# Moving the loads of a fused attention and FFN kernel behind the q transposes, and attention ahead of the FFN

## The chip, the cores and the metric

One core of one Trainium2 chip. The metric is the device time of one execution in microseconds, median of several runs; lower is better. Ratios below are computed as the mean time of one kernel's fast runs over that of the kernel before in the same rounds on the same chip, so they are not quite the ratio of the medians that are quoted beside them.

## The reference, cut to what matters

```python
# q, k, v: (8 batches, 8 heads, 576 tokens, 64); w_phi: (64, 128)
proj = x @ w_phi;  proj -= max(abs(proj), axis=-1)        # phi of q and of k
phi = concat([exp(proj), exp(-proj)])
kv = phi(k)^T v;  z = sum over tokens of phi(k)
x = (phi(q) kv) / (phi(q) z)                              # attention, 4608 tokens x 512
out = relu(x @ w_in)**2 @ w_out                           # FFN 512 -> 2048 -> 512
```

## The kernel before

The program has its own planner. It describes each piece of work as an operation with an engine, an estimated cost, a key (priority) and dependencies, runs a greedy list schedule over all engines once, and emits the instructions of each engine in the order found. On the chip every engine works through its own list in that fixed order; semaphores only guard data. **So a dependency that stands only in the plan (as on loads) changes an order, but the chip does not wait for it.**

```python
def load(key, kb, rows, fn, deps=(), bufs=()):            # HBM to SBUF, issued by GpSimd
    ...
    i = pl.op("pool", 780, key, fn, list(deps) + ..., bufs, lat=0)
    d = pl.op("dma", kb * 2.5, key, None, [i], bufs, lat=2600)

def xbar(key, kb, fn, deps=(), bufs=()):                  # DMA transpose, issued by SyncE
    i = pl.op("sp", 1300, key, fn, deps, bufs, lat=0)
    return pl.op("xb", kb * 6, key, None, [i], bufs, lat=2500)
```

For batches 2 to 7, k and q are loaded from the chip's memory (HBM) to the core's (SBUF) as they lie, and five DMA transposes each make kT and qT (for q from batch 1). The output x of attention is turned into xT, the FFN's input, by further DMA transposes, all from SyncE's one queue:

```python
nc.sync.dma_start_transpose(out=xt.t[:, u0 // 2 : (u0 + n) // 2, :], in_=...)   # kT, qT
nc.sync.dma_start_transpose(out=xT.t[:, tt], in_=xo.t)                         # xT
```

The K phase of a batch (phi of its k) costs VectorE, for each of two banks of PSUM, the memory that takes matmul results, in five groups, a reduce and a subtract (`mk`, `ksh`):

```python
def less(e, ...):
    amax(e)                                               # reduce: mk
    nc.vector.tensor_tensor(out=ksh..., in0=wv(e), in1=mk..., op=ALU.subtract)
```

FFN work is cut into 288 units (four 512-column matmuls each) whose keys are 0, 1, 2, ...; a batch of attention gets keys in a window of SPAN units that ends DUE units before the FFN needs it. NATT is how many of the 8 PSUM banks attention may hold; LEAD, a planner constant for pacing attention.

```python
NATT, LEAD, DUE, SPAN = 7, 3, 26, 36
def place(b):
    ...
    end = due[(NJ * b + NJ - 1) // 2 // 4] - DUE
    return lambda i: end - SPAN * (1 - i / 100)
...
attention(b, ... loads(b, last_x[b - 2][-2] if b > 3 else None), place(b))
```

Of the kernel before, what the change touches and what calls it, by code (L numbers as in the profile page):

```python
# [10 lines left out]
BF16 = mybir.dt.bfloat16  # L11
# [34 lines left out]
class Plan:  # L46
# [31 lines left out]
    def order(self):  # L78
        ready = {e: [] for e in sorted({o.eng for o in self.ops}, key=lambda e: (e != "x", e))}
        busy = {e: 0.0 for e in ready}  # L80
        rows = {e: None for e in ready}
        for o in self.ops:
            if o.n == 0:
                heapq.heappush(ready[o.eng], (o.key, o.seq, o))
        ev, now, done = [], 0.0, []

        def can(o):
            new = [x for x in o.bufs if x.slot is None]
            return all(x.can() and len(x.ring.free) >= sum(y.ring is x.ring for y in new)
                       for x in new)  # L90

        while True:
            for e, q in ready.items():
                if busy[e] > now:
                    continue
                skip = []
                while q:
                    it = heapq.heappop(q)
                    o = it[2]
                    if not can(o):  # L100
                        skip.append(it)
                        continue
                    for x in o.bufs:
                        if x.slot is None:
                            x.take()
                    o.start = now
                    end = now + o.cost
                    if o.rows is not None:
                        if rows[e] not in (None, o.rows):
                            end += self.SWITCH  # L110
                        rows[e] = o.rows
                    busy[e] = end
                    done.append(o)
                    same = [d for d in o.next if d.eng == e]
                    other = [d for d in o.next if d.eng != e]
                    for i, (t, what) in enumerate((
                            (end, ()), (end + 60, same), (end + o.lat, other),
                            (end + o.lat, None))):
                        heapq.heappush(ev, (t, 4 * o.seq + i, o, what))
                    break  # L120
                for it in skip:
                    heapq.heappush(q, it)
                if busy[e] <= now and e in self.idle and self.idle[e][2].start is None:
                    cost, fn, _ = self.idle[e]
                    o = Op()
                    o.eng, o.fn, o.start, o.cost, o.key = e, fn, now, cost(now), 1e9
                    busy[e] = now + o.cost
                    done.append(o)
                    heapq.heappush(ev, (busy[e], -len(done), o, ()))
            if not ev:  # L130
                break
            now = ev[0][0]
            while ev and ev[0][0] <= now:
                _, _, o, what = heapq.heappop(ev)
                if what is None:
                    for x in o.bufs:
                        x.left -= 1
                        if x.left == 0:
                            x.ring.free.append(x.slot)
                    continue  # L140
                for d in what:
                    d.n -= 1
                    if d.n == 0:
                        heapq.heappush(ready[d.eng], (d.key, d.seq, d))
        assert all(o.start is not None for o in self.ops)
        self.span = now
        return done
# [10 lines left out]
def kernel(  # L158
# [10 lines left out]
    nc = tc.nc  # L169
# [4 lines left out]
    P = 128  # L174
# [3 lines left out]
    M = U // 2  # L178
# [16 lines left out]
    wphi_f = sb.tile([P, Fd], F32, name="wphi_f")  # L195
    ones = sb.tile([P, Fd], BF16, name="ones")
    scrap = sb.tile([P, 8], F32, name="scrap")

    r_xk = ring("xk", 2, [P, U, D], BF16)
    r_xq = ring("xq", 2, [P, U, D], BF16)  # L200
# [16 lines left out]
    r_h2 = ring("h2", 30, [P, TCH], BF16)  # L217
    r_ot = ring("ot", 2, [P, DM], F32)

    NATT, LEAD, DUE, SPAN = 7, 3, 26, 36  # L220

    r_one = ring("one", 8, [P, 512], F32, ps)
    r_att = Ring(list(range(NATT)))
# [2 lines left out]
    pl = Plan()  # L226
# [15 lines left out]
    def pool(key, cost, fn, deps=(), bufs=()):  # L242
        return pl.op("pool", cost, key, fn, deps, bufs, lat=150 + MARGIN)

    queue, issues = [], []
# [8 lines left out]
    def load(key, kb, rows, fn, deps=(), bufs=()):  # L254



        n = (queue[-1][0] if queue else 0) + rows
        full = [d for m, d in queue if m >= n - 4096][:1]
        i = pl.op("pool", 780, key, fn, list(deps) + (full if n > 4096 else []), bufs, lat=0)  # L260
        issues.append(i)
        d = pl.op("dma", kb * 2.5, key, None, [i], bufs, lat=2600)
        queue.append((n, d))
        return d

# [75 lines left out]
    def attention(b, x, key):  # L341
# [4 lines left out]
        def transposes(xb, ld, xt, at):  # L346

            ops = []
            if b >= NPE or b and at:
                for u0, n in GRP:  # L350
                    def fn(u0=u0, n=n):
                        nc.sync.dma_start_transpose(
                            out=xt.t[:, u0 // 2 : (u0 + n) // 2, :],
                            in_=xb.t[:, u0 : u0 + n, :].rearrange("x u d -> x (u d)"),
                        )
                    ops.append(xbar(key(at), n * 16, fn, ld[0] + (x["v"][1][0] if b > 1 else []), [xb, xt]))
                return ops
            for u0, n in ((0, 16), (16, 16), (32, 4)) if b or at else GRP:
                w, = banks(1)

                def fn(u0=u0, n=n, w=w):
                    for i in range(n // 2):
                        nc.tensor.transpose(
                            out=tp(w)[:, i], in_=xb.t[:, u0 + 2 * i : u0 + 2 * i + 2, :]
                            .rearrange("x u d -> x (u d)"), identity=ident)
                kk = key(1 + u0 + 4 * at)
                p_ = pe(kk, 40 + n * 30, fn,
                        [o_id] + ld[0] + (ld[-1] if u0 + n > U // 2 else []), [w, xb, xt])
                ms = slice(u0 // 2, (u0 + n) // 2)
                if b or at:  # L370
                    o = dve(kk, n * 38, lambda w=w, n=n, ms=ms: nc.vector.tensor_copy(
                        out=xt.t[:, ms, :], in_=tp(w)[:, : n // 2]), [p_], [w, xt])
                else:
                    o = act(kk, n * 64, lambda w=w, n=n, ms=ms: nc.scalar.activation(
                        out=xt.t[:, ms, :], in_=tp(w)[:, : n // 2], func=ACT.Copy),
                        [p_], [w, xt])
                ops += [o] * (1 if not (b or at) else (n + 7) // 8)
            return ops

        tk = transposes(xk, lk, kT, 0)  # L380
        tq = transposes(xq, lq, qT, 1)


        va = [Buf(r_va), Buf(r_va)] if b == 0 else [Buf(r_va)] * 2
# [134 lines left out]
        for i, (g0, j0, nj) in enumerate(order_j):  # L519
# [117 lines left out]
            if hi_ == P and b == 0:  # L637
                w, = banks(1)

                def fn(w=w, xo=xo):  # L640
                    for kc in range(KC1):
                        nc.tensor.transpose(
                            out=tp(w)[:, kc], in_=xo.t[:, kc * P : (kc + 1) * P], identity=ident)
                p_ = pe(kk, 240, fn, parts, [w, xo, xT])

                def fn(w=w, xT=xT, tt=tt):
                    nc.scalar.activation(out=xT.t[:, tt], in_=tp(w)[:, :KC1], func=ACT.Copy)
                xT_ops[c].append(act(kk, 512, fn, [p_], [w, xT]))
                last_x.setdefault(b, []).append(xT_ops[c][-1])
            elif hi_ == P:  # L650
                def fn(xo=xo, xT=xT, tt=tt):
                    nc.sync.dma_start_transpose(out=xT.t[:, tt], in_=xo.t)
                deps = parts if nj == 2 else parts + xo_half.pop()
                xT_ops[c].append(xbar(kk, 128, fn, deps, [xo, xT]))
                last_x.setdefault(b, []).append(xT_ops[c][-1])
            else:
                xo_half.append(parts)

    xo_half, nds, last_x = [], [], {}


    h2 = {}
# [85 lines left out]

    spare = Buf(r_one, 7)
    pl.op("x", 0, 0, None, (), [spare])  # L750
    gated = []
    for b in range(B):
        n = len(issues)
        attention(b, x0 if b == 0 else x1 if b == 1 else loads(b, last_x[b - 2][-2] if b > 3 else None),
                  place(b))
        if b == 3:
            gated = issues[n:]
    o_end = pl.op("x", 0, 0, None, xT_ops[0][:1], [spare])
    pl.fill("pe", lambda now: 500 if now < 500 else 240 if now < 5500 else 125, warm, o_end)
    paced = [o for o in att if o.key > 8]  # L760
# [4 lines left out]
    for o in paced:  # L765
        n = int(o.key) - LEAD
        if 0 <= n < len(units):
            pl.after(o, att[n])

    for o in gated:  # L770
        pl.after(o, h2[1, 0, 0][2])
    with tc.manual_schedule():
        for o in pl.order():
            if o.fn is not None:
# [32 lines left out]
```

## Time and profile before

387.0 us (386.71 to 387.28). From the page of the profiled run: engine totals, then the span in 40 slices of 9.6 us (a digit is the busy share in tenths; PEclk is the granted TensorE clock, DMA the share of the 16 DMA engines).

```profile
span 384.8 us, 10484 instructions
PE 368.5 (96%) x4152; PEld 199.6 (52%) x4152; DVE 248.0 (64%) x554; ACT 244.1 (63%) x485; POOL 184.7 (48%) x310
PE   8899799999994999999999999999999999999994
DVE  2878977994693747894798468947893764233221
PEclk9999989999996999999999999999999999999999
DMA  8999994349989442389559563964311232112123
```

TensorE (PE) is the bottleneck. After start-up one hole is left, in the thirteenth slice, with a lower clock in it. The waits view of TensorE from 112 to 123 us (who waited for whom: us in total, times, longest) says for what:

```profile
PE one_163 L561 <- DMA qT_76<-xq_71: 3.2, 1, 3.2
PE one_157 L561 <- DMA qT_76<-xq_71: 1.6, 1, 1.6
```

L561 is a Q matmul of batch 3. The chain of waits from 100 to 125 us (start, duration, what) shows how it comes about:

```profile
104.41 1.21 DVE m_106 L565 x2
105.61 0.99 SPq L652
106.66 1.26 SPq L352
107.97 1.26 SPq L352
109.27 1.26 SPq L352
110.57 10.29 DMA qT_76<-xq_71
```

SyncE was held up by an xT transpose (L652) that needed VectorE's result. The q transposes (L352) came after it, and the last took 10.29 us. GpSimd's timeline gives the reason: at just that moment it issued the loads for batch 4, 3.5 MB in float32 (stored as 576 KB of bfloat16 each).

```profile
108.72 0.81 POOL L301 DMA_DIRECT2D xk_68<-in_k_dram  x1 [0.36 <-issue]
109.52 0.75 POOL L301 DMA_DIRECT2D xq_70<-in_q_dram  x1
110.25 0.76 POOL L301 DMA_DIRECT2D xv_72<-in_v_dram  x1
```

The two transposes issued before the loads (106.66, 107.97) landed after 2.48 and 2.46 us, the two after (109.27, 110.57) after 9.70 and 10.29 us. The windows view, in pieces, shows the clock around it (columns: window, its length, then busy us of PE, PEld, DVE, ACT, POOL, each with its count; granted clock; DMA share; GB/s):

```profile
118.00:121.00 3.00, 0.37 (x2) 0.19 (x2) 0.94 (x3) 0.34 (x1) 0.00 (x0) 0.50 1.22 198
121.00:124.00 3.00, 3.00 (x11) 0.86 (x12) 0.42 (x1) 0.56 (x2) 0.37 (x2) 0.50 1.36 239
124.00:125.00 1.00, 1.00 (x4) 0.40 (x3) 0.00 (x0) 0.86 (x2) 0.00 (x0) 0.62 0.69 250
125.00:128.00 3.00, 3.00 (x25) 1.38 (x24) 0.79 (x2) 1.97 (x6) 1.26 (x2) 1.00 0.34 74
```

### The profile page before, as it was taken

The numbers are of one execution on the slowest core, as the hardware profiler recorded it, in microseconds if no ns is written. First come the engines' busy times: TensorE is split into PE (matmuls) and PEld (weight loads), VectorE is DVE, ScalarE is ACT, GpSimd is POOL, SyncE is SP. The second block draws the span as 40 slices with busy tenths as digits, with TensorE's granted clock in tenths as the row PEclk, the third lists the DMA queues.
The fourth block names the chain that finished last, engine by engine and source line by source line (L and its number), as shares of the span: only waits on it lengthen the run. The fifth ranks groups of instructions, "written<-read, shape, count | busy, mean of one in ns | idle before, by whom it ended". The sixth has DMA issues, their size and how long they took to land.

```text
span 384.8 us, 10484 instructions
## 1 busy us (share of the span) xinstructions
PE 368.5 (96%) x4152; PEld 199.6 (52%) x4152; DVE 248.0 (64%) x554; ACT 244.1 (63%) x485; POOL 184.7 (48%) x310
## 2 busy tenths in 40 slices
PE   8899799999994999999999999999999999999994
PEld 7788656544551455545544544455445454444442
DVE  2878977994693747894798468947893764233221
ACT  4795879568943796588649775887588653333300
POOL 8543846439940696297556656575445320000000
PEclk9999989999996999999999999999999999999999
DMA  8999994349989442389559563964311232112123
GB/s 124 211 208 204 168 188 87 75 75 210 101 126 206 89 57 48 72 139 151 111 89 200 80 115 63 200 121 95 70 27 31 49 64 53 44 27 55 28 61 75
DMA packets 70720, 40.39 MB, mean 105 GB/s; under 512 B 51088, under 2 KB 65552, under 8 KB 70672
## 3 DMA queue, kind: packets, MB, share of 16 engines
q1 hardware_dynamic: 55360, 21.38, 31.3%
q0 software_dynamic: 15312, 18.35, 29.1%
q8 instruction: 32, 0.52, 0.6%
q14 instruction: 16, 0.13, 0.1%
HBM read 36.77 MB, written 9.44 MB: 120 GB/s over the span
## 4 chain that ended last, share of the span: by engine, by line
PE 84%; DVE 7%; DMA 3%; ACT 2%; POOL 1%; SPq 1%; issue 1%; DVEq 0%
PE one_163 L704 6%; PE one_164 L675 5%; PE one_161 L704 5%; PE one_159 L704 5%; PE one_162 L675 4%; PE one_157 L675 4%; PE one_159 L675 4%; PE one_163 L675 4%; PE one_157 L704 4%; PE one_162 L704 4%; PE one_160 L675 3%; PE one_161 L675 3%; PE one_160 L704 3%; PE one_164 L322 3%; PE one_158 L675 3%; DMA qT_76<-xq_71 3%
## 5 line engine op out<-in xcount | busy, mean ns | idle before, releaser
L675 PEld LDWEIGHTS <-win 128*128 128x128 bf16 x704 | 59.2, 98 | 55.6 <-issue 5.2
L322 PE MATMUL one_164<-ones 128*128 128x128 bf16 x274 | 20.8, 233 | 1.1 <-DVE scrap L280 1.1
L574 POOL COPY mq_107<-m_104 64x4 f32<-64x4 f32 x52 | 9.6, 184 | 20.9 <-DVE m_104 L565 16.6
L322 PEld LDWEIGHTS <-ones 128*128 128x128 bf16 x274 | 17.6, 105 | 2.4 <-DVE scrap L280 1.1
L574 POOL COPY mq_108<-m_105 64x4 f32<-64x4 f32 x46 | 8.5, 184 | 11.7 <-DVE m_105 L565 10.3
L406 PEld LDWEIGHTS <-kT_74 64*128 64x128 bf16 x288 | 8.2, 94 | 8.8 <-issue 7.2
L574 POOL COPY mq_109<-m_106 64x4 f32<-64x4 f32 x46 | 8.5, 184 | 8.3 <-DVE m_106 L565 6.8
L680 ACT ACTIVATE hr_124<-one_160 128x512 bf16<-128x512 f32 x9 | 5.4, 596 | 8.6 <-PE one_160 L675 8.1
L683 POOL TENSOR_TENSOR h_141<-hr_123 128x512 bf16<-128x512 bf16 x4 | 4.2, 1039 | 11.6 <-ACT hr_123 L680 10.2
L675 PE MATMUL one_163<-xT_118,win 128*128 128x128 bf16 (+2 forms) x88 | 9.4, 253 | 0.3 <-ACT em_111 L581 0.2
L680 ACT ACTIVATE hr_123<-one_163 128x512 bf16<-128x512 f32 x9 | 5.3, 592 | 6.3 <-PE one_163 L675 5.7
L680 ACT ACTIVATE hr_122<-one_162 128x512 bf16<-128x512 f32 x9 | 5.4, 597 | 5.4 <-PE one_162 L675 5.3
L565 DVE TENSOR_REDUCE m_104<-one_162 128x4 f32<-128x512 f32 x6 | 4.1, 688 | 7.0 <-ACT hr_122 L680 4.9
L461 POOL TENSOR_TENSOR va_90<-xv_72,va_90 128x512 bf16<-128x512 bf16 (+1 forms) x5 | 6.2, 1244 | 5.0 <-ACT kph_80 L448 4.4
L561 PEld LDWEIGHTS <-qT_76 64*128 64x128 bf16 x144 | 4.4, 94 | 7.5 <-DMA qT_76<-xq_71 5.2
L683 POOL TENSOR_TENSOR h_143<-hr_122 128x512 bf16<-128x512 bf16 x4 | 4.2, 1044 | 8.3 <-ACT hr_122 L680 8.3
L532 PEld LDWEIGHTS <-wphi_61 64*128 64x128 bf16 x160 | 4.8, 94 | 6.2 <-issue 5.0
L435 ACT ACTIVATE kph_79<-ksh_88 128x1024 bf16<-128x1024 f32 x5 | 5.3, 1055 | 4.3 <-DVE ksh_88 L427 4.2
L610 PEld LDWEIGHTS <-qph_97 128*128 128x128 bf16 (+1 forms) x104 | 5.4, 101 | 4.7 <-issue 1.7
L680 ACT ACTIVATE hr_123<-one_161 128x512 bf16<-128x512 f32 x8 | 4.8, 604 | 4.3 <-PE one_161 L675 3.6
L565 DVE TENSOR_REDUCE m_105<-one_164 128x4 f32<-128x512 f32 (+1 forms) x7 | 4.5, 646 | 4.6 <-PE one_161 L561 4.1
L680 ACT ACTIVATE hr_123<-one_164 128x512 bf16<-128x512 f32 x9 | 5.4, 596 | 3.1 <-PE one_164 L675 3.1
(1001 smaller groups left out, 1365.2 us busy)
## 6 DMA issues: line engine op xcount, KB each, us to landing
out_dram<-ot_155 SPq DMA_DIRECT2D x36, 128.0 KB, 2.4
out_dram<-ot_156 SPq DMA_DIRECT2D x36, 128.0 KB, 2.4
xk_69<-in_k_dram POOLq DMA_DIRECT2D x4, 576.0 KB, 6.8
xq_71<-in_q_dram POOLq DMA_DIRECT2D x4, 576.0 KB, 9.9
xv_73<-in_v_dram POOLq DMA_DIRECT2D x4, 576.0 KB, 12.9
win<-in_moe_w_in_dram POOLq DMA_DIRECT2D x1, 2048.0 KB, 18.4
wout<-in_moe_w_out_dram POOLq DMA_DIRECT2D x1, 2048.0 KB, 31.0
xk_68<-in_k_dram POOLq DMA_DIRECT2D x3, 576.0 KB, 7.4
```

What stands on the lines that cost most here:

```text
L322: nc.tensor.matmul(out=r_one.tiles[7][:, :P], lhsT=ones, rhs=ones, start=True, stop=True)
L406: nc.tensor.matmul(out=w[e].t[:, i * Fd : (i + 1) * Fd], lhsT=kT.t[r, u0 // 2 + i, :], rhs=wphi2[r, :], start=True, stop=True)
L435: nc.scalar.activation(out=t.t[:, :, : n // 2, :].rearrange("x e i f -> x e (i f)"), in_=ksh.t[:, :, : n // 2, :].rearrange("x e i f -> x ...
L461: v_.tensor_tensor(out=y.t[:, u0 : u0 + n, :D], in0=xv.t[:, u0 : u0 + n, :], in1=y.t[:, u0 : u0 + n, D].to_broadcast([P, n, D]), op=ALU.mult)
L532: nc.tensor.matmul(out=o[bk][:, r], lhsT=wphi2[x, :], rhs=qT.t[x, m : m + nj, :].rearrange("x m (hi p) -> x m hi p", hi=2), start=True, st ...
L565: d1 = [dve(kk, nj * 256, lambda w=w, m0=m0, nj=nj, bk=bk: nc.vector.tensor_reduce(out=m0.t[:, bk, : 2 * nj], in_=w[bk].t[:, : nj * 256].r ...
L574: nc.gpsimd.tensor_copy(out=mq.t[lo + jj * 64 : lo + jj * 64 + 64, :, :, hi], in_=m0.t[hi * 64 : hi * 64 + 64, :, : 2 * nj].rearrange("x b ...
L610: nc.tensor.matmul(out=nd(slice(0, D + 1))[:, z], lhsT=qg[s].t.rearrange("f pr hi p -> f (pr hi p)")[:, h * (hi_ - lo) : (h + 1) * (hi_ - ...
L675: nc.tensor.matmul(out=w.t[:, y * n : (y + 1) * n], lhsT=win[:, kc, mc * P : (mc + 1) * P], rhs=xT.t[:, a:z, kc, :], start=(kc == 0), stop ...
L680: o = act(key - 4, TCH, lambda: nc.scalar.activation(out=r.t, in_=w.t, func=ACT.Relu), [p_], [w, r])
L683: o = pool(key - 4, 1050, lambda: nc.gpsimd.tensor_tensor(out=t.t, in0=r.t, in1=r.t, op=ALU.mult), [o], [r, t])
L704: nc.tensor.matmul(out=w.t, lhsT=h2[c, mc, tt][0].t[:, h2[c, mc, tt][1] :][:, :P], rhs=wout[:, mc, :], start=(mc == 0), stop=(mc == KC2 - 1))
```

## The change: its intent, and the diff

Loads should not fall beside the q transposes, and FFN input should be ready earlier. GpSimd, which issues the loads, first reads a few elements of the end of qT of the batch before, so the chip itself holds the loads back. Attention is due 34 units ahead instead of 26, in a window of 28 instead of 36 (so it starts at the same unit), with 6 banks instead of 7. Loads are planned at 3 ns per KB instead of 2.5.

```diff
-    NATT, LEAD, DUE, SPAN = 7, 3, 26, 36
+    NATT, LEAD, DUE, SPAN = 6, 3, 34, 28
@@ load
-        d = pl.op("dma", kb * 2.5, key, None, [i], bufs, lat=2600)
+        d = pl.op("dma", kb * 3, key, None, [i], bufs, lat=2600)
@@ attention, after the transposes of k and q are planned
+        if b:
+            d = pl.op("x", 1000, key(2), None, tq)
+            gates[b] = pool(key(2), 100, lambda: nc.gpsimd.tensor_copy(
+                out=gate, in_=qT.t[:1, M - 1, P - 8 :]), [d], [qT])
@@ the batch loop
-        attention(b, ... loads(b, last_x[b - 2][-2] if b > 3 else None), place(b))
-        if b == 3:
-            gated = issues[n:]
+        attention(b, ... loads(b, gates.get(b - 1) if b > 2 else None), place(b))
...
-    for o in gated:
-        pl.after(o, h2[1, 0, 0][2])
```

The cuts leave out the bookkeeping of `last_x`, the tile `gate`, and a renaming in the planner without effect.

More of the change, by code (lines that the diff above doesn't have):

```diff
@@ L106, in order @@
                     o.start = now
-                    end = now + o.cost
+                    end, lat = now + o.cost, o.lat
                     if o.rows is not None:
@@ L116, in order @@
                     for i, (t, what) in enumerate((
-                            (end, ()), (end + 60, same), (end + o.lat, other),
-                            (end + o.lat, None))):
+                            (end, ()), (end + 60, same), (end + lat, other),
+                            (end + lat, None))):
                         heapq.heappush(ev, (t, 4 * o.seq + i, o, what))
@@ L197 @@
     scrap = sb.tile([P, 8], F32, name="scrap")
+    gate = sb.tile([1, 8], BF16, name="gate")
     r_xk = ring("xk", 2, [P, U, D], BF16)
@@ L648, in attention @@
                 xT_ops[c].append(act(kk, 512, fn, [p_], [w, xT]))
-                last_x.setdefault(b, []).append(xT_ops[c][-1])
             elif hi_ == P:
@@ L654, in attention @@
                 xT_ops[c].append(xbar(kk, 128, fn, deps, [xo, xT]))
-                last_x.setdefault(b, []).append(xT_ops[c][-1])
             else:
                 xo_half.append(parts)
-    xo_half, nds, last_x = [], [], {}
+    xo_half, nds, gates = [], [], {}
     h2 = {}
@@ L750 @@
     pl.op("x", 0, 0, None, (), [spare])
-    gated = []
     for b in range(B):
-        n = len(issues)
-        attention(b, x0 if b == 0 else x1 if b == 1 else loads(b, last_x[b - 2][-2] if b > 3 else None),
+        attention(b, x0 if b == 0 else x1 if b == 1 else loads(b, gates.get(b - 1) if b > 2 else None),
                   place(b))
-        if b == 3:
-            gated = issues[n:]
     o_end = pl.op("x", 0, 0, None, xT_ops[0][:1], [spare])
```

## The prediction

> **What bounds the kernel now.** TensorE: the page gives it 96% of the 384.8 us span, and 84% of the chain of waits. From 190 to 310 us a batch of attention with its 32 FFN units takes about 40 us, with no TensorE gap over 0.25 us; that part only moves if waits are added. After start-up one large loss is left. The waits view has TensorE idle 3.2 + 1.6 us (116 to 121 us in the timeline) before the last Q matmuls of batch 3, until a transposing DMA has written qT. The chain view gives the cause: these transposes issue at 106.7 to 110.6 us, behind two xT transposes; GpSimd issues the loads of batch 4 at 108.7 to 110.3; the two transposes issued after 108.7 land after 9.7 and 10.3 us, the two before after 2.46 to 2.48. The Trainium skill, "DMA: Bandwidth & Descriptors", "Issuing engines are not separate DMA queues", says that DMAs of different engines share the same 16 DMA engines and interleave; these durations agree. After the gap the clock is halved for about 6.8 us (windows view: 0.75 in 115-121, 0.73 in 121-128), some 3.4 us more. The skill's "TensorE: Matmul & The Clock Gate", Part 1, says that an idle window drops the clock to 4/8; the trace agrees. Sum: 4.8 + 3.4 = 8.2 us.
>
> **What the change does.** (1) GpSimd reads the end of q^T of batch b-1 before it issues the loads of batch b (from 3 on), so the chip keeps loads off those transposes. Cost: a tiny copy per batch (comparable 64x4 copies take 0.18 us), and GpSimd's wait where transposes land later than planned. (2) Attention starts at the same FFN unit but is due 8 units earlier (28 units instead of 36): batches no longer overlap, xT has some 8 to 10 us more slack, q transposes should no longer queue behind late xT transposes. (3) Attention gets 6 PSUM banks instead of 7. (4) Loads are planned 20% longer. No matmul is removed.
>
> **On the critical path.** All 8.2 us are, and I expect nearly all to go. Against it: VectorE is busy 9.4 to 9.9 of 10 us in the K phases (windows 80-90, 150-160, 200-210, 240-250 us; a 512-column reduce takes 0.68 us). With fewer units and one bank less I estimate waits on VectorE of 0.2 to 1 us each, 1 to 2 us in all. Start-up (idle 2.6 us between 43 and 48 us, then half clock for 3.4 us) is reordered: plus or minus 2 us. Gate stalls of GpSimd: 0 to 2 us each, mostly hidden by the buffers behind it.
>
> **Prediction:** 379.8 us, 374.5 to 386.0 in 8 of 10 cases; faster by over 2% 0.43, within 2% 0.52, slower 0.05.
>
> **What would show it right or wrong.** Right: no q transpose of batches 2 to 7 lands after more than about 5 us; TensorE never waits on qT; clock 1.00 from 70 to 375 us; loads of batch 4 and later begin only after the last q transpose of the batch before has landed. Wrong: TensorE's waits on VectorE (ksh, m) exceed 3 us in sum; GpSimd sits several us at the gate and TensorE then waits on h2; or FFN unit 24 (73 us before) moves by over 3 us.
>
> **What would make it wrong.** A new collision elsewhere (xT transposes still overlap loads, at 9 to 11 us each), early batches delayed by the gate for batch 1, or a reordered start-up that saves more than I count.

## The result, and the profile after

383.58 us (383.19 to 384.28, 4 runs) against 387.0 (386.71 to 387.28): ratio 0.9914, 95% interval 0.9897 to 0.9931. Faster by 0.9%, a little under half of the 1.9% predicted, and within the predicted range of times. The profiled run was the slowest of the four (384.28 us). Its page (this trace's names carry no buffer numbers, and the same statements stand a few lines lower in the program):

```profile
span 382.5 us, 10585 instructions
PE 366.7 (96%) x4194; PEld 200.9 (53%) x4194; DVE 247.7 (65%) x554; ACT 244.4 (64%) x485; POOL 185.9 (49%) x317
PE   8989999978999999999999999999999999999994
DVE  1857894899279738973699488956895843333221
PEclk9998999999999999999999999999999999999998
DMA  7999994257944595459665946495631422112123
```

The hole in the thirteenth slice is gone and so is the lower clock there. A new hole stands in the ninth and tenth slices, where VectorE is full. The waits view of TensorE from 80 to 94 us:

```profile
PE one L616 <- DVE one L627: 1.4, 1, 1.4
PE one L679 <- DVE ksh L433: 1.3, 2, 0.7
PE one L538 <- DVE ot L715: 0.3, 1, 0.3
PE one L567 <- DVE ksh L433: 0.2, 1, 0.2
```

The windows view for 80 to 90 us, the kernel before first, then the changed one; TensorE drops from 9.59 to 7.20 us busy while VectorE stays full:

```profile
80.00:90.00 10.00, 9.59 (x67) 3.96 (x66) 9.58 (x20) 8.05 (x11) 6.69 (x8) 1.00 0.58 100
```

```profile
80.00:90.00 10.00, 7.20 (x67) 3.55 (x65) 9.64 (x22) 5.88 (x7) 1.87 (x3) 1.00 0.55 112
```

GpSimd's timeline around the first gate that matters:

```profile
88.13 1.04 POOL L687 TENSOR_TENSOR h<-hr 128x512 bf16<-128x512 bf16 x1 [10.00 <-ACT hr L684]
89.11 0.18 POOL L386 COPY gate<-qT 1x8 bf16<-1x8 bf16 x1
89.26 1.03 POOL L687 TENSOR_TENSOR h<-hr 128x512 bf16<-128x512 bf16 x1
90.24 0.81 POOL L302 DMA_DIRECT2D xk<-in_k_dram  x1
```

The gate has no wait in brackets: the last q transpose had landed at 86.59 us, 2.5 us earlier. This holds for all six batches; the margin is 2.2 to 4.4 us. No recorded q transpose of batches 2 to 7 takes more than 3.9 us (before: 10.3), and no xT transpose more than 4.5 us (before: 11.3). The loads now meet k transposes instead: eight of these took 6.8 to 8.4 us (before: up to 7.3), and no wait of TensorE on kT is listed. So loads and transposes still collide, but in transposes for whose result TensorE does not wait.

To see where time went, I took from both traces the time from each matmul's start to the next one's, less what the Trainium skill ("TensorE: Matmul & The Clock Gate", "Wait — 56ns, not 53.3ns?") gives for N columns on a warm array, N / 2.4 GHz + 2.5 ns. The trace agrees: four 512-column matmuls start 0.864 us after the four before, 216 ns each. Matmuls on 64 rows, which run in pairs, count half; warm-up matmuls on constants, which only keep TensorE busy, count as lost. The sum of what is left, from the first matmul to the last, in us, rounded:

| stretch, us | before | after | difference |
|---|---|---|---|
| 0 to 60 | 30.6 | 31.0 | +0.3 |
| 60 to 80 | 2.5 | 2.7 | +0.1 |
| 80 to 100 | 3.1 | 6.5 | +3.4 |
| 100 to 130 | 9.4 | 3.0 | -6.4 |
| 130 to 180 | 5.6 | 5.1 | -0.4 |
| 180 to 220 | 4.3 | 7.0 | +2.7 |
| 220 to the end | 10.4 | 8.3 | -2.1 |
| sum | 65.9 | 63.6 | -2.3 |

The sum is the difference of the two spans (384.8 and 382.5). The expected gain was realised between 100 and 130 us, and half of it was given back between 80 and 100 us. The other two larger differences, +2.7 and -2.1, nearly cancel; no experiment was made on them.

### The profile page after: what moved, and what is told of

It is laid out like the page before. It is cut to its first block, busy times and chain, and to the rows that moved or that the text cites. A ratio compares the mean times of both kernels' runs of the same rounds, so it can differ in the third digit from the quotient of the medians.

```text
span 382.5 us, 10585 instructions
## 1 busy us (share of the span) xinstructions
PE 366.7 (96%) x4194; PEld 200.9 (53%) x4194; DVE 247.7 (65%) x554; ACT 244.4 (64%) x485; POOL 185.9 (49%) x317
## 4 chain that ended last, share of the span: by engine, by line
PE 74%; DMA 11%; DVE 9%; issue 3%; POOL 1%; DVEq 0%; POOLq 0%
PE one L708 32%; PE one L679 25%; DMA wout<-in_moe_w_out_dram 8%; PE one L616 5%; PE one L500 5%; DVE mk L423 4%; DVE ksh L433 3%; PE one L538 3%; DMA xv<-in_v_dram 2%; PE one L567 2%; PE one L412 2%; DVE ot L715 1%; DVE xo L638 1%; POOL va L467 1%; DVE one L627 1%
## 5 line engine op out<-in xcount | busy, mean ns | idle before, releaser
L687 POOL TENSOR_TENSOR h<-hr 128x512 bf16<-128x512 bf16 x112 | 115.2, 1042 | 83.7 <-ACT hr L684 81.7
L679 PE MATMUL one<-xT,win 128*128 128x512 bf16 (+2 forms) x704 | 144.2, 341 | 2.8 <-DVE ksh L433 2.8
L708 PE MATMUL one<-wout,h 128*128 128x512 bf16 x576 | 144.5, 380 | 0.8 <-DMA wout<-in_moe_w_out_dram 0.5
L684 ACT ACTIVATE hr<-one 128x512 bf16<-128x512 f32 x144 | 84.5, 603 | 67.7 <-PE one L679 59.8
L548 ACT ACTIVATE qph<-one 128x512 bf16<-128x512 f32 (+1 forms) x160 | 77.9, 563 | 19.5 <-PE one L538 19.3
L708 PEld LDWEIGHTS <-h 128*128 128x128 bf16 x576 | 51.0, 98 | 56.6 <-issue 1.4
L441 ACT ACTIVATE kph<-ksh 128x1024 bf16<-128x1024 f32 (+1 forms) x70 | 64.8, 964 | 19.7 <-DVE ksh L433 19.2
L571 DVE TENSOR_REDUCE m<-one 128x4 f32<-128x512 f32 (+1 forms) x80 | 47.9, 630 | 41.7 <-PE one L567 24.9
L423 DVE TENSOR_REDUCE mk<-one 128x4 f32<-128x512 f32 (+1 forms) x80 | 49.7, 627 | 8.3 <-PE one L412 8.2
L433 DVE TENSOR_TENSOR ksh<-one,mk 128x512 f32<-128x512 f32 (+1 forms) x70 | 44.7, 638 | 3.8
L616 PEld LDWEIGHTS <-qph 128*128 128x128 bf16 (+1 forms) x640 | 29.7, 100 | 22.2 <-issue 11.3
L616 PE MATMUL one<-kv_sb,qph 128*128 128x65 bf16 (+1 forms) x640 | 36.9, 196 | 1.5 <-DVE one L627 1.4
```

The source lines that it names most:

```text
L423: nc.vector.tensor_reduce(out=mk.t[:, e, ms], in_=wv(e), axis=AX.X, op=ALU.max, apply_absolute_value=True)
L433: nc.vector.tensor_tensor(out=ksh.t[:, e, : n // 2, :], in0=wv(e), in1=mk.t[:, e, ms].to_broadcast([P, n // 2, Fd]), op=ALU.subtract)
L441: nc.scalar.activation(out=t.t[:, :, : n // 2, :].rearrange("x e i f -> x e (i f)"), in_=ksh.t[:, :, : n // 2, :].rearrange("x e i f -> x ...
L548: nc.scalar.activation(out=t.t.rearrange("f pr hi p -> f (pr hi p)")[:, : nj * 512].rearrange("f (r b c) -> f b r c", r=2, b=2)[:, bk], in ...
L571: d1 = [dve(kk, nj * 256, lambda w=w, m0=m0, nj=nj, bk=bk: nc.vector.tensor_reduce(out=m0.t[:, bk, : 2 * nj], in_=w[bk].t[:, : nj * 256].r ...
L616: nc.tensor.matmul(out=nd(slice(0, D + 1))[:, z], lhsT=qg[s].t.rearrange("f pr hi p -> f (pr hi p)")[:, h * (hi_ - lo) : (h + 1) * (hi_ - ...
```

## The experiments

Three theories stood at one time or another. **A**, mine after the result: the gate removes the collision, and the tighter window with one bank less gives time back as waits on VectorE. **B**, the rival: any edit redraws the whole greedy order, and the result is the luck of the draw. **C**, formed after the first four runs: a DMA transpose in flight beside the loads takes about 10 us, and *which* transposes stand there, and whether TensorE needs their result soon, is decided by the planned order; the gate's wait itself is idle. The times of the kernel before beside these runs were 387.42, 386.99 and 387.9 us.

### 1. The gate alone

Due, window, banks and planned loads as before: `NATT, LEAD, DUE, SPAN = 7, 3, 26, 36`, `kb * 2.5`, with the gate.

> The kernel before with the gate alone (GpSimd reads the end of qT of batch b-1, loads of batch b hang on it from batch 3); window, banks and planned load cost as before. Theory A (the gate removes the collision of 8.2 us, the tighter window with one bank less gives some 4 to 6 us back as waits on VectorE): 378.5 to 381 us, faster than the changed kernel's 383.6; no q transpose of batches 2 to 7 takes over 5 us. Theory B (any edit redraws the order that the greedy plan gives to all engines, and the time is the luck of that draw): anywhere from 380 to 390 us, with waits in places that neither kernel had.

392.18 us (391.73 to 393.68), ratio 1.0132 (1.009 to 1.0175): slower than before. Theory A falls in the form in which it was written: TensorE waits on no q transpose after start-up (the longest took 5.6 us), and yet 5 us are lost. The waits view of TensorE from 70 to 130 us has one new line, and SyncE's and GpSimd's timelines show the collision, now with xT:

```profile
PE one L679 <- DMA xT<-xo: 8.8, 2, 5.0
```

```profile
73.28 3.53 SPq L657 DMA_TRANSPOSE xT<-xo  x2
```

```profile
74.35 0.18 POOL L386 COPY gate<-qT 1x8 bf16<-1x8 bf16 x1 [0.66 <-DMA qT<-xq]
74.87 0.80 POOL L302 DMA_DIRECT2D xk<-in_k_dram  x1 [0.34 <-PE one L616]
75.67 0.75 POOL L302 DMA_DIRECT2D xq<-in_q_dram  x1
```

The second of these xT transposes, issued at 75.62 us, landed after 10.13 us, and the FFN waited for it. The same again at 122 us.

### 2. Everything but the gate

The changed constants in the kernel before (`6, 3, 34, 28` and `kb * 3`), loads on their old dependencies.

> The changed kernel without the gate: the loads hang on the old dependencies, everything else (28 units, due 34, 6 banks, loads planned longer) is as in the change. Theory A: at least one q transpose of 9 us or more in flight beside loads; if it is on TensorE's chain, 388 to 392 us, since the waits on VectorE stay (about 5 us) and the collision is back. Theory B: no fixed relation, the collision may be absent because the order moved; 380 to 390 us.

391.21 us (388.04 to 393.16), ratio 1.0082 (1.0009 to 1.0156). Slow q transposes are back (9.7, 10.8 and 8.4 us beside the loads of 112.5 to 114.0 us), and TensorE waits 6.3 us at 120.8 us, but on the xT transpose that SyncE issued after them.

```profile
PE one L675 <- DMA xT<-xo: 6.3, 1, 6.3
```

The changed kernel's waits on VectorE stand here too, 3.2 us between 80 and 93 us, so with both losses in it this run came out where A expected it. So neither half of the change works alone: each is slower than before (this one by little more than the noise), and both together are faster.

### 3. The gate in the plan only

```diff
-            gates[b] = pool(key(2), 100, lambda: nc.gpsimd.tensor_copy(...), [d], [qT])
+            gates[b] = pl.op("x", 0, key(2), None, [d], [qT])
```

> The changed kernel with GpSimd's read of qT taken out: the plan still puts the loads behind the q transposes, the chip no longer enforces it. If the wait that the chip keeps matters, some q transpose of batches 2 to 7 lands after more than 5 us and TensorE waits on qT, 386 us or more. If only the order matters: within 1.5 us of the changed kernel's 383.6 us and no slow q transpose, because the loads stand behind other GpSimd work that is as late.

Fast runs 385.04 to 386.4 us, ratio 0.9959 (0.9912 to 1.0005). Inconclusive: the edit also takes 0.1 us of planned GpSimd time away, which redraws the order. Run 5 asks the same without touching the order.

### 4. Gate and longer planned loads, old window and banks

`NATT, LEAD, DUE, SPAN = 7, 3, 26, 36` in the changed kernel.

> The changed kernel with the window, due and banks of before (36 units, due 26, 7 banks); gate and longer planned loads stay. Theory A: 378 to 381 us, waits of TensorE on VectorE between 70 and 220 us drop from about 6 us to under 2 us. Theory B: 380 to 390 us; VectorE waits stay, at other places.

397.99 us (394.28 to 399.39), ratio 1.0261 (1.0197 to 1.0325), the opposite of what A expected. TensorE waits 3.4 us at 160 us and 5.7 us at 238 us on xT, whose transposes took 8.5 to 10.9 us beside the loads; and six waits on VectorE between 80 and 87 us come back (0.4 to 0.9 us each) although window and banks are the old ones. B's range, 380 to 390 us, was missed here and in runs 1 and 2 as well.

### 5. The changed kernel with its order, without the wait

```diff
-            gates[b] = pool(key(2), 100, lambda: nc.gpsimd.tensor_copy(...), [d], [qT])
+            gates[b] = pool(key(2), 100, lambda: None, [d], [qT])
```

> The changed kernel, with every operation of every engine in the same order, but GpSimd's read of qT is not emitted: the slot in the plan stays, the wait on the chip goes. In the profile of the changed kernel the read never waits (the last q transpose of batches 2 to 7 has landed 2.3 to 4.4 us before it starts), so theory C (the gate works only through the order; the wait itself is idle) expects the ratio of the changed kernel, 0.991, within 0.003. If the wait is worth something on the chip: 0.995 or more, with a q transpose of over 5 us.

383.01 us (382.32 to 384.1), ratio 0.9894 (0.9866 to 0.9921), the changed kernel's 0.9914 within the stated 0.003. No q transpose over 3.8 us. In the changed kernel the wait that the chip keeps is worth nothing measurable; what is left of the gate is the order that it gives to the plan, in which the loads stand behind the q transposes.

### 6. The collision by itself

The kernel before, its order untouched, but batch 4's loads are not issued (wrong result).

```diff
             def fn(a, z, buf=buf, rows=rows):
+                if b in (4,):
+                    return
```

> The kernel before in exactly its order, but the three loads of batch 4 are not issued (its tiles keep the data of batch 2: a wrong result on purpose). Prices the collision by itself. Theory A/C: the q transposes of batch 3 take 2.5 us, TensorE no longer waits on qT at 116 to 121 us, no half clock after it: 8.2 us less, ratio 0.977 to 0.983 (378.5 to 380.5 us). If the stall has another cause (the late issue of the transposes behind xT): under 3 us saved, ratio above 0.992.

380.31 us (380.01 to 380.74), ratio 0.982 (0.9789 to 0.985): 0.018 x 387 = 7.0 us (5.8 to 8.2 by the interval). TensorE no longer waits on qT between 100 and 130 us, and the clock is full there. The four q transposes that stood at 106.7 to 110.6 us are issued as late as before, at 107.4 to 111.3 us, and take 2.5 to 4.1 us, so lateness behind xT was not the cause. The window that was nearly empty, to be set against 0.37 us busy at clock 0.50 above:

```profile
118.00:121.00 3.00, 3.00 (x16) 1.30 (x14) 2.44 (x6) 3.00 (x7) 0.37 (x2) 1.00 0.41 90
```

The collision is what the profile said, and this prices all of it, that of the two xT transposes beside these loads (11.3 and 9.4 us before) included.

### 7. The xT collisions by themselves

The same edit in the kernel of run 1, with `if b in (3, 4)` (wrong result).

> The kernel with the gate alone (392.2 us), in exactly its order, but the loads of batches 3 and 4 are not issued (wrong result on purpose). In its profile TensorE waited 5.0 us at 81 us and 3.8 us at 122 us for xT, whose transposes took 9 to 10 us beside those loads, each with half clock for 6.8 us after it. Theory C (the gate moves the collision from the q transposes to the xT transposes): xT transposes of 2.5 us there, both waits and both half clocks gone, 13 to 16 us less, ratio to before 0.97 to 0.98 (376 to 379 us). If xT is late for another reason: under 5 us saved.

380.02 us (379.3 to 380.23), ratio 0.9806 (0.977 to 0.9842); run 1 had 1.0132. The difference of 0.0326 is 12.6 us, just under the 13 to 16 expected. No wait on xT is left from 70 to 130 us. This and run 6 are the evidence for theory C: with no edit to any order, taking the loads away takes the waits away, whichever transposes stood beside them.

### 8. The new wait by itself

The changed kernel, its order untouched, without the reduce in the K phase of batch 2. It uses the maximum of an earlier batch instead, so it computes something else.

```diff
                 def less(e, ...):
-                    amax(e)
+                    if b != 2:
+                        amax(e)
```

> The changed kernel in exactly its order, but the reduce of the K phase of batch 2 is not emitted (10 of 20 VectorE instructions there, about 0.6 us each; wrong result on purpose). In the changed kernel TensorE waits 3.3 us in all on VectorE between 82 and 93 us. If VectorE limits that stage: those waits go, 2.5 to 4 us less, ratio to before 0.981 to 0.985 (about 380.3 us). If it is PSUM banks or the order: under 1 us saved.

380.47 us (379.85 to 380.89), ratio 0.9822 (0.979 to 0.9853). Against the changed kernel (0.9914) that is 3.6 us, against run 5 (0.9894) 2.8 us, by the intervals uncertain by some 1.4 us. The windows view for 80 to 90 us of this kernel, against 7.20 and 9.64 us above:

```profile
80.00:90.00 10.00, 8.75 (x76) 3.94 (x74) 7.55 (x18) 9.06 (x12) 4.58 (x7) 1.00 0.58 109
```

VectorE limits this stage and costs about 3 us. The wait in front of L616 and those on `ksh` between 70 and 100 us are gone; 1.1 us of waiting on xT came up in their place.

### 9 and 10. Which part of the change makes the new wait?

Run 9 is the changed kernel with `kb * 2.5`, run 10 with `NATT` 7.

> The changed kernel with loads planned as before (2.5 ns per KB instead of 3); gate, 28 units, due 34 and 6 banks stay. Which part makes TensorE wait 3.3 us on VectorE in the K phase of batch 2? So far the wait stood in every kernel with longer planned loads (the changed one, without the gate, and with the old window: 3 to 4 us between 80 and 93 us) and in none with the old loads. If the longer loads alone make it: no such waits, and 379 to 382 us unless xT collides. If the short window makes it as well: 3 to 6 us of such waits again, and 384 us or more; a wait on xT of 4 us or more is then likely too, since this edit redraws the order (theory C: it shows as an xT transpose of 9 us or more beside loads).

> The changed kernel with 7 PSUM banks for attention as before, the rest as in the change. If the sixth bank makes the waits on VectorE in the K phase of batch 2 (FFN and attention fighting for banks that VectorE frees): under 1 us of them, 380 to 382 us. If they come from the work of batches 1 and 2 falling together: 3 us or more stay, 384 to 389 us.

Run 9: 398.94 us (397.46 to 401.31), ratio 1.0307 (1.0238 to 1.0376). The waits on VectorE are there without the longer loads (seven between 82 and 91 us, 0.4 to 0.9 us each), and the xT collision returns (4.4 us at 124 us). Run 10: 386.38 us (385.93 to 386.98), ratio 0.9978 (0.9921 to 1.0034): with 7 banks six waits on VectorE between 80 and 88 us remain (0.3 to 1.0 us each, 4.0 us in all), so they do not need the cut to six banks. Nor do they need the tighter window (run 4) or the longer loads (run 9, which keeps both six banks and the tighter window). Yet run 11 below has a window of 26, loads planned at 2.75 and none of these waits. So no one constant is their cause; what makes the order that has them stays open.

### 11 and 12. A faster version

The gate and its mechanism as in the change, with constants from a search; the settings were ranked by a replay of the planned order on the host in which a transpose beside loads takes 10 us. MARGIN is extra latency, in ns, that the plan allows between engines. The replay only chose the candidates; the times are the chip's.

```diff
-    NATT, LEAD, DUE, SPAN = 6, 3, 34, 28
+    NATT, LEAD, DUE, SPAN = 7, 3, 32, 26      # run 12: 7, 4, 32, 25
-    MARGIN = 300
+    MARGIN = 200
-        d = pl.op("dma", kb * 3, key, ...)
+        d = pl.op("dma", kb * 2.75, key, ...) # run 12: 2.6
```

> A try at a faster kernel: the gate, 7 banks, due 32, window 26, loads planned at 2.75 ns per KB and the planner's extra latency at 200 ns instead of 300. Chosen from a search with a replay of the plan in which transposes beside loads take 10 us; it promises no xT or qT transpose that TensorE waits for and no pile-up of batches 1 and 2 on VectorE. Theory C: no wait of TensorE on xT or qT over 1 us and under 2 us on VectorE in 70 to 100 us, 376 to 381 us. If theory C misses a cause: 383 us or more.

> A second try of the same kind: the gate, 7 banks, lead 4, due 32, window 25, loads planned at 2.6 ns per KB, extra latency 200 ns. Same expectation: no wait of TensorE on xT or qT over 1 us, 375 to 381 us; 383 us or more if theory C misses a cause.

Run 11: **378.51 us** (377.65 to 379.93), ratio 0.9776 (0.9706 to 0.9847), correct, and below both kernels; the changed kernel's interval, 0.9897 to 0.9931, lies above it. Run 12: 382.02 us (381.17 to 382.69), ratio 0.9863 (0.9807 to 0.992). Run 12 had been expected at 375 to 381 us, a shade faster than run 11, and misses that; why it is 3.5 us slower is not shown. So the replay is a sieve and not a clock. The page of run 11:

```profile
PE   8989799999999999999999899999999999999994
DVE  1968966995789687868578577957696763333221
PEclk9999999999999999999999999999999999999998
```

No wait of TensorE on qT or xT reaches 0.2 us in either; the longest transposition of q or xT after start-up takes 4.3 us in run 11. VectorE's digits are flatter: between 70 and 100 us TensorE has no listed wait on it. No run with a fixed order says what either improvement is worth here.

## Why the prediction was right or wrong

- **Right: the place of the loss and its cause.** Run 6 removed it with no edit to the order. "TensorE never waits on qT", "no q transpose of batches 2 to 7 lands after more than about 5 us" and "clock 1.00 from 70 to 375 us" all came true, as did the loads' place behind the last q transpose. FFN unit 24 moved by 2.0 us (73.0 to 71.0), inside the stated 3.
- **Mis-sized: the gain of 8.2 us.** It is 7.0 us (run 6), though the interval, 5.8 to 8.2, just reaches it. The term "some 3.4 us more" for the halved clock charged all 6.8 us of half clock. TensorE sat idle in much of that, where a slow clock costs nothing: the windows above give 0.37 + 3.00 us busy at 0.50 and about 0.76 us of the next (clock 0.62), 4.1 us in all, so 2.1 us lost. 4.8 + 2.1 = 6.9, and the stretch from 100 to 130 us gained 6.4.
- **Mis-sized, and the main miss: "1 to 2 us in all" for waits on VectorE.** This is the step that failed. The prediction said that K phases would suffer, and named a sum over 3 us as a sign against it. From 60 us on, these waits sum to 5.0 us in the waits view, against 0.6 before. (In the whole run it is 5.7 against 3.7, the first wait of all, on a constant, left out in both: the kernel before was already past the 3 us, in start-up, so that sign could not tell.) One K phase alone, batch 2's, costs 2.8 to 3.6 us (run 8). A further 2.7 us is lost from 180 to 220 us, where the trace shows 0.9 us of waits on `ksh` and 0.9 us whose cause it does not show; that part was not tested. The arithmetic seems to close on the two that were, 387.0 less 7.0 plus about 3 is 383, measured 383.6, but in part by luck: it leaves out these 2.7 us and the 2.1 us gained after 220 us, which nearly cancel.
- **Wrong in the reason: "fewer units and one bank less".** Neither is needed. With seven banks the waits stay (run 10), and with the old window and seven banks, under longer planned loads, they come too (run 4).
- **Wrong: that the chip's wait does the work.** "The chip keeps loads off those transposes" describes a wait that is never waited for (run 5). The gate acts by moving the loads in the order.
- **Missed: that the parts are not additive.** The prediction named xT transposes beside loads as a risk, but counted the gate's gain as secure. The gate alone costs 1.3% and the rest alone 0.8%, because each moves the loads onto another transpose that TensorE needs soon (for the gate alone run 7 shows it; for the rest it is read from the trace, and waits on VectorE are part of it). Of the kernels between the two, only the one with both leaves qT and xT clear of the loads.

Theory B is not refuted but narrowed: edits do redraw the order, and a single constant moved the time by 4% (run 9 against the changed kernel), but in the two cases that were tested with the order fixed, the difference between draws came from a collision that can be named.

## What to carry to other kernels

When a wait in a static schedule has a cause in DMA traffic, price it by leaving the suspected transfer out with every order kept: that separates the transfer from the reshuffle which any edit of a planner brings. Before counting a gain from moving a transfer, list what else will be in flight at its new place and who needs that within the next 10 us. And charge a half clock only for the time in which the engine is busy.

## What the Trainium skill lacked or had wrong

- "DMA: Bandwidth & Descriptors", "Rules for kernel authors", says of a transpose that "next to ordinary DMAs" it "needs nothing". For correctness these runs agree; for time they do not: 2.4 to 2.5 us alone; beside three loads 9.7 and 10.3 us in the kernel before, and in runs 1, 2 and 4 after start-up mostly 7 to 11 us, at most 13.8. The page gives an effective bandwidth for a transpose, but a duration neither alone nor beside loads.
- The same page's "Issuing engines are not separate DMA queues" says that such DMAs share the 16 engines and interleave, which fits; it does not say that a small transfer then takes about as long as the large ones beside it. The loads of that moment took 7.4, 9.9 and 12.8 us.
- "TensorE: Matmul & The Clock Gate", Part 1, gives half clock after an idle window of about 3.4 us, and further down tells of a kernel whose clock fell through many short idle times; it does not say how idle a window has to be. In the kernel before the clock was halved for 3.4 us from 49.7 us on, after 3.4 us (46.27 to 49.68) with TensorE busy 1.77 us and no single gap over 1.04 us. So a window that was only about half idle was enough here.
